# Batch 0's first layer and rows as streams of the scheduler, one bank fewer bound by attention, and a choice of engine for relu and for rows' copies

## The chip, the cores and the metric

The kernel runs on one core of a Trainium2 chip. The core has a matrix engine (TensorE, PE in the profile, with its weight load PEld), VectorE (DVE), ScalarE (ACT), GpSimd (POOL), and SyncE (SP), which here only sends DMAs. The metric is the device time of one execution in microseconds; shorter is better. The kernel before takes 310.22 us, the median of three runs from 309.73 to 310.73.

## The reference

Eight batches of eight heads, 576 positions, 64 features per head. First an attention with 32 landmarks (means of 18 neighbouring positions), whose inverse is found by six iterations; then, over the heads put side by side, a normalisation and a two-layer block with a residual:

```python
q_lm = q.reshape(B, H, m, S // m, D).mean(axis=3)      # k_lm alike, m = 32
A, Bm, C = sm(q, k_lm), sm(q_lm, k_lm), sm(q_lm, k)    # scaled softmax
Z = Bm.T / (norm1(Bm) * norminf(Bm) + 1e-6)
for _ in range(6):
    Z = 2 * Z - Z @ Bm @ Z
x = A @ Z @ C @ v                                      # then [B, S, 512]
xn = (x - mean(x)) / sqrt(var(x) + 1e-6) * g_ln
out = x + relu(xn @ w_ch1) @ w_ch2                     # 512 -> 2048 -> 512
```

## The kernel before

**Tiling.** A unit is four heads of one batch, so a batch has two. Per batch there are four kinds of TensorE work. *Attention* makes landmarks (`spread`, L805), scores, six iterations (`iterate`, L644) and the small products zt and zc. The *first layer* (`First`, L1077) never forms xn @ w1 from x: `product_of_heads` (L1085) multiplies zt by a quarter of w1 into two banks, VectorE or ScalarE evacuates them to `m16`, and each of 16 `chunk`s (L1108) multiplies `m16` by the exponentials `ea` into `psh`, from which relu writes the hidden activations `hT`. *Rows* (`rows_of`, L658) compute x itself, 128 positions at a time, into the tile `xblk`, of which twelve exist. The *second layer* (`second_layer`, L1151) accumulates 16 matmuls per block of 128 rows; `finish_block` (L1139) multiplies by the reciprocal deviation `rstd`, adds x, and the result is stored. Batches have 4.5 blocks, so `keep_tail` copies a half block into the next batch's `hT`.

**Weights.** w1 and w2 arrive in eight pieces each. w1 is scaled by g when it is cast (`scale_w1`, L351; by GpSimd or ScalarE), w2 is cast by GpSimd. The mean of x is taken out through w1: `less_mean` multiplies w1 by -1/512, which gives `less`; for batches 0 and 1 it is added while m is evacuated on VectorE, and `center_w1` later adds it to w1 for good.

**Order.** The program is straight-line. Every engine runs its own instructions in program order, so the order is decided when the program is written out. `Clock` (L72) models when each engine is free and when each tile is written. `run` (L1256) holds three generators, `attentions`, `first_layers` and `second_layers`. Each yields the time from which its next piece could start; the first in this order that is ready by now plus 60 ns goes next, else the earliest. Before each step `help_out` (L1190) hands out loads, GpSimd casts, VectorE's jobs for coming batches (`turn`, `add_up`, `turn_sums`), statistics (`measure`) and deviations (ScalarE), by how soon the engine is free; `LEAD` (L1188) is 700 ns. Attention of the first batch, and the whole of batch 0's first layer with its rows, the sums of w1, batch 1's preparation and blocks 0 and 1 of the second layer, are instead written out by hand at the end (L1304 to L1372), with fixed places by chunk number m. There, `warm` writes filler matmuls whose results nobody reads.

**PSUM.** `ps2` has two buffers of two banks each, which attention and `psh` share. Four more banks are handed out by `Banks` (L383) in rotation: `take` uses one, `hold` keeps it until `release`, and `next(k)` is the time when k of them are idle. By line 1355, `banks.order.remove(3)`, bank 3 leaves the rotation after batch 0's chunk 14, and `attention2` (L865) uses it for scores and iterations of all later batches.

**Engines.** `sooner` (L476) takes ScalarE or VectorE, whichever would end sooner by the model. Relu (L1115) and the copies of rows (L672) always go to ScalarE. Of a unit's q and k, the sums over positions come either from VectorE (`add_up`, for tiles named in `by_dve`) or from four adds on GpSimd while it casts, followed by a short `turn_sums` on VectorE.

## Time and profile before

| | us |
|---|---|
| median of 3 runs | 310.22 |
| the profiled execution | 311.25 |
| its span, first to last instruction | 309.5 |
| SyncE's issue of w2's eight pieces | 26.45 to 34.67 |
| first relu of batch 0, of batch 1 (start) | 27.97, 69.11 |
| end of the last relu | 281.22 |

The page splits the span into engines' busy shares, 40 slices, queues, the chain that ended last, and groups of instructions. A row of the timeline reads: start, length, engine, line, operation, output<-inputs, shape, count, and in brackets the idle time before it and what ended it. All scheduled operations stand under a helper's line (L221, L227), so they are told apart by tile names. The costliest groups, with busy us, mean ns, and the idle time ahead:

```
L227 PE MATMUL bank<-w,hT 128*128 128x512 f16 (+1 forms) x592 | 145.3, 376 | 2.9 <-DVE m L221 1.4
L221 ACT ACTIVATE hT<-psh 128x576 f16<-128x576 f32 x128 | 79.5, 655 | 27.6 <-PE psh L227 26.4
L227 PE MATMUL psh<-ea,m 128*128 128x288 f16 x512 | 81.9, 295 | 6.0 <-ACT hT L221 4.3
```

A matmul's length includes its latency; in a stream the 512-column ones follow each other every 0.216 us.

### The profile page before, as it was taken

The page shows a single profiled execution, that of the slowest core. Times are in us where ns is not written, and L with a number is a line of the kernel's source. Part 1 is how long each engine was busy: PE and PEld are TensorE (multiplying, and loading weights), DVE is VectorE, ACT ScalarE, POOL GpSimd, SP SyncE. Part 2 cuts the span into 40 slices and gives each one's busy share as a digit, 9 for nine tenths or more (in the row PEclk, how much of TensorE's full clock was granted, in tenths as well). Part 3 has the DMA queues.
Part 4 walks back from the last instruction along what each step waited for, and adds up shares of the span by engine and source line. Part 5 has one row for each costly group of instructions (what it writes and reads, how often), then busy time and mean ns, then how long its engine had stood idle before and what let it go on. Part 6 is the DMA issues. An engine that isn't in the chain of part 4 may idle for free.

```text
span 309.5 us, 8189 instructions
## 1 busy us (share of the span) xinstructions
PE 282.5 (91%) x3420; PEld 151.2 (49%) x3420; DVE 176.7 (57%) x388; ACT 173.4 (56%) x306; POOL 126.8 (41%) x156
## 2 busy tenths in 40 slices
PE   8988889979898999998899989789897999999995
PEld 8633554435543564544555544346443555465444
DVE  2645976979878877698758365544245221221112
ACT  2664855347753886369988746657552664473000
POOL 4387656999636999289920026100030000100000
PEclk9965999968999999999999999999999899999999
DMA  7999999979526699807801001210111111211343
GB/s 251 392 388 351 369 293 351 284 269 331 176 77 176 186 370 275 231 19 194 242 2 35 22 18 36 68 34 9 29 36 35 36 34 40 66 34 36 70 92 75
DMA packets 23485, 46.66 MB, mean 151 GB/s; under 512 B 2324, under 2 KB 2584, under 8 KB 23448
## 3 DMA queue, kind: packets, MB, share of 16 engines
q1 hardware_dynamic: 23288, 46.02, 48.6%
q8 instruction: 26, 0.43, 0.6%
q10 hardware_dynamic: 160, 0.13, 0.2%
q14 instruction: 11, 0.09, 0.1%
HBM read 36.70 MB, written 9.44 MB: 149 GB/s over the span
## 4 chain that ended last, share of the span: by engine, by line
PE 61%; DMA 17%; ACT 8%; DVE 5%; POOL 4%; issue 3%; SPq 1%; ACTq 0%; POOLq 0%
PE bank L227 40%; PE psh L227 16%; DMA wstg<-in_moe_w_ch_dram 8%; DMA out_dram<-xblk 4%; DMA stg<-in_q_dram 3%; ACT hT L221 3%; ACT xblk L221 2%; DVE xblk L221 2%; PE psd L227 2%; POOL asum L221 2%; DMA stg<-in_k_dram 2%; PE pscv L227 1%; ACT ec L221 1%; PE psec L227 1%; SPq L1047 1%
## 5 line engine op out<-in xcount | busy, mean ns | idle before, releaser
L227 PE MATMUL bank<-w,hT 128*128 128x512 f16 (+1 forms) x592 | 145.3, 376 | 2.9 <-DVE m L221 1.4
L221 ACT ACTIVATE hT<-psh 128x576 f16<-128x576 f32 x128 | 79.5, 655 | 27.6 <-PE psh L227 26.4
L227 PE MATMUL psh<-ea,m 128*128 128x288 f16 x512 | 81.9, 295 | 6.0 <-ACT hT L221 4.3
L227 PEld LDWEIGHTS <-hT 128*128 128x128 f16 x592 | 55.3, 98 | 55.5 <-issue 7.5
L227 PEld LDWEIGHTS <-m 128*128 128x128 f16 x512 | 49.2, 100 | 35.2 <-issue 12.3
L221 DVE SCALAR_TENSOR_TENSOR xblk<-bank,rstd,xblk 128x512 f32<-128x512 f32 (+1 forms) x37 | 27.1, 734 | 49.5 <-PE bank L227 48.1
L221 POOL TENSOR_TENSOR ea<-ea,lns 128x576 f16<-128x576 f16 x14 | 17.8, 1283 | 46.5 <-ACT lns L221 46.5
L221 POOL CAST nat<-stg 128x1152 f16<-128x1152 f32 x28 | 32.5, 1178 | 6.5 <-DVE xT L221 3.9
L221 POOL CAST natv<-stg 128x1152 f16<-128x1152 f32 x16 | 18.6, 1190 | 35.0 <-PE pscv L227 25.1
L221 ACT COPY xblk<-bank 128x512 f32<-128x512 f32 (+1 forms) x40 | 21.8, 592 | 19.3 <-DMA out_dram<-xblk 10.1
L221 DVE BATCH_NORM_STATS2 six<-xblk 128x6 f32<-128x512 f32 x36 | 24.4, 676 | 7.7 <-ACT xblk L221 7.6
L221 DVE CAST m<-bank 128x512 f16<-128x512 f32 x19 | 13.1, 691 | 24.4 <-PE bank L227 24.4
L221 DVE TENSOR_REDUCE part<-xT 128x32 f16<-128x576 f16 x32 | 22.9, 748 | 0.4
L221 ACT CAST m<-bank 128x512 f16<-128x512 f32 x29 | 16.4, 585 | 10.4 <-PE bank L227 10.4
L221 DVE STREAM_TRANSPOSE xT<-nat 128x576 uint32<-128x576 uint32 x28 | 21.5, 767 | 0.0
L227 PE MATMUL bank<-w,zt 64*32 64x512 f16 x256 | 15.9, 407 | 4.3 <-ACT xblk L221 4.0
L221 POOL COPY hT<-hT 128x1024 f16<-128x1024 f16 x4 | 4.1, 1037 | 37.8 <-PE bank L227 37.8
L227 PE MATMUL bank<-zcbd,ea 128*128 128x256 f16 (+1 forms) x80 | 15.6, 294 | 3.9 <-DVE xblk L221 2.0
L221 ACT ACTIVATE lns<-psd 128x576 f32<-128x576 f32 x16 | 10.3, 645 | 11.5 <-PE psd L227 11.4
L221 DVE SCALAR_TENSOR_TENSOR st<-st,bank 128x128 f16<-128x128 f16 (+2 forms) x36 | 11.1, 309 | 8.4 <-PE bank L227 8.4
L221 POOL TENSOR_TENSOR asum<-asum 128x256 f32<-128x256 f32 (+1 forms) x24 | 14.5, 604 | 1.9
L221 POOL TENSOR_TENSOR asum<-nat 128x512 f32<-128x512 f16 x12 | 14.5, 1207 | 1.0
(111 smaller groups left out, 262.3 us busy)
## 6 DMA issues: line engine op xcount, KB each, us to landing
stg<-in_q_dram SPq DMA_DIRECT2D x16, 576.0 KB, 6.0
stg<-in_k_dram SPq DMA_DIRECT2D x16, 576.0 KB, 6.9
out_dram<-xblk SPq DMA_DIRECT2D x70, 128.0 KB, 2.4
wstg<-in_moe_w_ch_dram SPq DMA_DIRECT2D x16, 512.0 KB, 8.0
stg<-in_v_dram SPq DMA_DIRECT2D x9, 576.0 KB, 7.7
stg<-in_v_dram SPq DMA_DIRECT2D x14, 288.0 KB, 7.8
out_dram<-xblk ACTq DMA_DIRECT2D x2, 64.0 KB, 2.2
out_dram<-xblk SPq DMA_DIRECT2D x2, 64.0 KB, 1.9
```

The costliest lines, as they stand in the source:

```text
L221: return lambda *args, **kw: keep(getattr(self.engine, op)(*args, **kw))
L227: keep(nc.tensor.matmul(o, l, r, start=start, stop=stop, tile_position=(rb, cb), skip_group_check=(skip or cb != 0)))
L1047: (nc.scalar if both and i else nc.sync).dma_start(out=to, in_=half)
```

## The change

Five things. (1) Batch 0's first layer is a generator (`first_layer0`) in `first_layers`, its rows are a fourth stream of `run` (between first and second layers), batch 1's preparation and attention go the way of all others, and blocks 0 and 1 of the second layer (`blocks_0_and_1`) are a piece of the second-layer stream, open once ten chunks are out. It waits for `hT` by the model, not for w2. The part written by hand goes. (2) `attention2` takes a bank from the rotation when it begins and releases it after its sixth iteration. Rows of batches from 1 on ask for two idle banks. (3) Relu, from batch 1 on, and those batches' copies of rows go to VectorE when the model has ScalarE later. (4) VectorE's lead is 400 ns until batch 1 is ready; statistics take precedence once a first layer has sent four chunks; deviations and the end of a block wait, by the model, for their inputs; k2's and k3's sums of batches 3 and 4 go to GpSimd, whose cast then also waits for a free `s16`. (5) In the opening a piece of w1 is scaled by VectorE one iteration later instead of by ScalarE, and there are more filler matmuls.

```diff
     heads, ready, multiplied, cast_v = {}, set(), {0}, {0}
+    rows0 = []
...
         st, bmT = softmax_of(psb, W)
-        warm(3, 256)
+        warm(4, 256)
...
-        cinv, _ = gram_of(p1([P, 4, W * LM], "psse"), st, bmT, W, lambda: warm(1, 256))
+        cinv, _ = gram_of(p1([P, 4, W * LM], "psse"), st, bmT, W, lambda: warm(2, 256))
...
-        warm(3, 256)
+        warm(4, 256)
         yield "gram"
...
         banks.release(*banks.held)
+        rows0.append(rows_of((0,), ea, zcbd_buf[0:2]))
         yield "zc"
-        yield from rows_of((0,), ea, zcbd_buf[0:2])
...
                 rows = ds(pb, n)
-                yield lambda: max(banks.next(), 0.0 if j in x_blk else xpool.next("xblk"),
+                yield lambda: max(banks.next(2 if b else 1), 0.0 if j in x_blk else xpool.next("xblk"),
                                   clock.at(ea[U * i], ea[U * i + 1], zcbd[U * i], zcbd[U * i + 1]))
...
                        zcbd[U * i + u][:].rearrange("p h d -> p (h d)"), cb=pb)
-                scalar.copy(xb[rows, :], psy[rows, :])
+                (sooner(512, clock.at(psy)) if b else scalar.copy)(xb[rows, :], psy[rows, :])
                 t0 += n
...
                 return max(clock.at(self.stg[i]), clock.idle(natv_buf[b % NV]))
-            return max(clock.at(self.stg[i]), nat.next("nat"))
+            return max(clock.at(self.stg[i]), nat.next("nat"),
+                       0.0 if nm + str(w) in self.by_dve else asm.next("s16"))
...
         W = len(units)
-        b3 = banks.tiles[3]
+        ecT, mine = {}, []
         def p1(shape, name):
-            return banks.view(3, shape)
-        psb = p1([P, W, LM], "psb")
-        ecT = {}
+            if not mine:
+                banks.hold([P, 512])
+                mine.append(banks.last)
+            return banks.view(mine[0], shape)
         for y in range(W // 2):
             pair = (2 * y, 2 * y + 1)
-            yield lambda: max(clock.idle(b3) if y == 0 else 0.0, ps2.next("p2", 2), aexp.next("e", 4),
+            yield lambda: max(0.0 if mine else banks.next(), ps2.next("p2", 2), aexp.next("e", 4),
                               clock.at(c.lm_tile[y], *[xT["k", w] for w in pair]))
+            if y == 0:
+                psb = p1([P, W, LM], "psb")
             for w in pair:
...
                 it += 1
+                if it == 6:
+                    banks.release(mine[0])
             else:
...
             o = self.hT[:, m, ds(64 * (self.b % 2), S)].rearrange("p (a t) -> p a t", a=2)
-            act(o, psh[:, :, 0:HS], AF.Relu)
+            at = clock.at(psh)
+            if self.b and max(clock.free["Activation"], at) + 650 > max(clock.free["DVE"], at) + 810:
+                dve.tensor_scalar(out=o, in0=psh[:, :, 0:HS], scalar1=0.0, scalar2=None, op0=ALU.max)
+            else:
+                act(o, psh[:, :, 0:HS], AF.Relu)
...
         l1 = First(b)
+        if b == 0:
+            yield from first_layer0(l1)
+            return
         yield lambda: max(banks.next(2), mprod.next("m16"), clock.at(l1.zt))
...
             l1.chunk(m)
+            if m == 3:
+                begun_first[0] = b
             if m % 4 == 0 and m < 12:
...
             asm.unpin(l1.zt)
+    chunks0 = [0]
+    def first_layer0(l1):
+        l1.product_of_heads(0)
+        scale_w1(5, 1, scalar)
+        for m in range(MCH):
+            yield lambda: max(ps2.next("p2"), clock.at(l1.m16[m // 4], *l1.ea))
+            l1.chunk(m)
+            chunks0[0] = m + 1
+            if m == 0:
+                scale_w1(7, 1, scalar)
+            if m in (2, 6):
+                f = 2 if m == 2 else 3
+                for c in range(KCH):
+                    yield lambda: max(0.0 if c else banks.next(), clock.at_key(w1_16[:, c, ts(f, 512)]))
+                    if c == 0:
+                        psf_of[f] = banks.hold([P, 512])
+                        mine = banks.last
+                    MM(psf_of[f][:], lesser[:], w1_16[:, c, ts(f, 512)], start=(c == 0),
+                       stop=(c == KCH - 1))
+                scalar.copy(less(f), psf_of.pop(f)[:])
+                banks.release(mine)
+            if m in (1, 5, 9):
+                yield lambda: max(banks.next(2), mprod.next("m16"))
+                l1.product_of_heads(m // 4 + 1)
...
+    def finished(b):
+        while b not in rstds:
+            if blocks_done.get(b) == 4 + b % 2:
+                yield lambda: clock.at(stats_of[b])
+                deviations(b)
+            elif unmeasured:
+                measure()
+            else:
+                yield lambda: 0.0 if b in rstds or unmeasured else NEVER
+        yield lambda: clock.at(rstds[b])
+    def blocks_0_and_1():
+        yield lambda: banks.next(2) if chunks0[0] >= 10 else NEVER
+        accs = []
+        for u in range(2):
+            accs.append((banks.hold([P, DM]), banks.last))
+        for m in range(MCH):
+            yield lambda: clock.at_key(hTs[0][:, m, 0:P]) if chunks0[0] > m else NEVER
+            for u in range(2):
+                MM(accs[u][0], hTs[0][:, m, ts(u, P)], w2_16[:, m, :],
+                   start=(m == 0), stop=(m == MCH - 1))
+        yield from finished(0)
+        for u in range(2):
+            finish_block(0, u, accs[u][0])
+            banks.release(accs[u][1])
     def second_layer(b):
         hT = hTs[b]
+        if b == 0:
+            yield from blocks_0_and_1()
         blocks = range(4 + b % 2) if b else (2, 3)
...
                        start=(m == 0), stop=(m == MCH - 1))
-                while b not in rstds:
-                    if blocks_done.get(b) == 4 + b % 2:
-                        deviations(b)
-                    elif unmeasured:
-                        measure()
-                    else:
-                        yield lambda: 0.0 if b in rstds or unmeasured else NEVER
+                yield from finished(b)
                 if u == blocks[-1]:
...
     sets = [Coming((1,), ("k0", "k1", "q0", "q1"))]
-    sets += [Coming(bs, [f"k{w}" for w in range(U * len(bs))]) for bs in ((2,), (3, 4), (5, 6), (7,))]
-    LEAD = 700
+    sets += [Coming(bs, [f"k{w}" for w in range(U * len(bs))] if bs != (3, 4) else ["k0", "k1"]) for bs in ((2,), (3, 4), (5, 6), (7,))]
+    def lead():
+        return 700 if 1 in ready else 400
...
                     break
-            if clock.free["DVE"] <= now + LEAD:
+            if clock.free["DVE"] <= now + lead():
                 mine = [c for c in sets if c.jobs][:1]
-                if unmeasured and current[0] >= group_of(unmeasured[0])[0]:
+                if unmeasured and begun_first[0] >= group_of(unmeasured[0])[0]:
                     measure()
...
                     begun = -1
-                elif mine and mine[0].job_ready() <= now + LEAD:
+                elif mine and mine[0].job_ready() <= now + lead():
                     mine[0].next_job()
...
             b = current[0]
-            if b not in rstds and blocks_done.get(b) == 4 + b % 2:
+            if (b not in rstds and blocks_done.get(b) == 4 + b % 2
+                    and clock.at(stats_of[b]) <= now + 200):
                 deviations(b)
...
-    current = [0]
+    current, begun_first = [0], [0]
     def attentions():
-        yield from a1
-        for c in sets[1:]:
+        for c in sets:
             for y in range(len(c.units) // 2):
...
     def first_layers():
-        for b in range(1, B):
-            yield lambda: 0.0 if (b in ready and current[0] == b - 1
-                                  and (b <= LAST_WHOLE or len(centered) == 4)) else NEVER
+        for b in range(B):
+            yield lambda: 0.0 if b == 0 or (b in ready and current[0] == b - 1
+                                            and (b <= LAST_WHOLE or len(centered) == 4)) else NEVER
             yield from first_layer(b)
             first_done.add(b)
+            if b == 0:
+                keep_tail(0)
...
     def run():
-        streams = [attentions(), first_layers(), second_layers()]
+        streams = [attentions(), first_layers(), rows0[0], second_layers()]
         waits = [next(g) for g in streams]
...
             at = [w() if w else 2 * NEVER for w in waits]
-            k = next((k for k in range(3) if at[k] <= now), None)
+            k = next((k for k in range(4) if at[k] <= now), None)
             if k is None:
...
         next(a0)
-        if it == 0:
-            scale_w1(1, 1, scalar)
+        if it == 1:
+            scale_w1(1, 1, dve)
         if it < 2:
-            warm(2, 192)
+            warm(3, 256)
+        elif it < 4:
+            warm(1, 256)
         if it == 3:
...
     next(a0)
-    l1 = First(0)
-    l1.product_of_heads(0)
-    scale_w1(5, 1, scalar)
-    accs = [banks.view(u, [P, DM]) for u in range(2)]
-    def blocks_0_and_1(m):
-        for u in range(2):
-            MM(accs[u][:], hTs[0][:, m, ts(u, P)], w2_16[:, m, :],
-               start=(m == 0), stop=(m == MCH - 1))
-    a1 = attention2((1,), b1)
-    for m in range(MCH):
-        l1.chunk(m)
-        if m == 0:
-            scale_w1(7, 1, scalar)
-        if m == 1:
-            l1.product_of_heads(1)
-        if m == 2:
-            less_mean(2)
-        if m == 5:
-            l1.product_of_heads(2)
-        if m == 6:
-            less_mean(3)
-        if m == 8:
-            l1.product_of_heads(3)
-        if m == 9:
-            banks.order, banks.held = [3, 2, 0, 1], {0, 1}
-        if m in (7, 8, 10, 11, 12, 13):
-            next(a0, None)
...
-        if m == 13:
-            b1.spread(0)
-        if m == 14:
-            assert not b1.jobs
-            banks.order.remove(3)
-            next(a1)
-            next(a1)
-        help_out()
-        if m >= 10:
-            blocks_0_and_1(2 * (m - 10))
-            blocks_0_and_1(2 * (m - 10) + 1)
-    keep_tail(0)
-    next(a1)
-    for m in range(12, MCH):
-        blocks_0_and_1(m)
...
     run()
```

More of the change, by code (lines that the diff above doesn't have):

```diff
@@ L1317 @@
     next(a0)
-    l1 = First(0)
-    l1.product_of_heads(0)
-    scale_w1(5, 1, scalar)
-    accs = [banks.view(u, [P, DM]) for u in range(2)]
-    def blocks_0_and_1(m):
-        for u in range(2):
-            MM(accs[u][:], hTs[0][:, m, ts(u, P)], w2_16[:, m, :],
-               start=(m == 0), stop=(m == MCH - 1))
-    a1 = attention2((1,), b1)
-    for m in range(MCH):
-        l1.chunk(m)
-        if m == 0:
-            scale_w1(7, 1, scalar)
-        if m == 1:
-            l1.product_of_heads(1)
-        if m == 2:
-            less_mean(2)
-        if m == 5:
-            l1.product_of_heads(2)
-        if m == 6:
-            less_mean(3)
-        if m == 8:
-            l1.product_of_heads(3)
-        if m == 9:
-            banks.order, banks.held = [3, 2, 0, 1], {0, 1}
-        if m in (7, 8, 10, 11, 12, 13):
-            next(a0, None)
-        if 2 <= m < 10:
-            b1.next_job()
-            if b1.jobs and b1.jobs[0][0] == b1.add_up and b1.jobs[0][2]:
-                b1.next_job()
-        if m == 13:
-            b1.spread(0)
-        if m == 14:
-            assert not b1.jobs
-            banks.order.remove(3)
-            next(a1)
-            next(a1)
-        help_out()
-        if m >= 10:
-            blocks_0_and_1(2 * (m - 10))
-            blocks_0_and_1(2 * (m - 10) + 1)
-    keep_tail(0)
-    next(a1)
-    for m in range(12, MCH):
-        blocks_0_and_1(m)
-    while 0 not in rstds:
-        if unmeasured:
-            measure()
-        deviations(0)
-    for u in range(2):
-        finish_block(0, u, accs[u])
-    banks.release(0, 1)
     run()
```

## The prediction

> **What bounds the kernel now.** I first read the busy shares by engine and the granted clock over 40 slices, then the chain of work that ended last.

> ```profile
> PE 282.5 (91%) x3420; PEld 151.2 (49%) x3420; DVE 176.7 (57%) x388; ACT 173.4 (56%) x306; POOL 126.8 (41%) x156
> PEclk9965999968999999999999999999999899999999
> PE 61%; DMA 17%; ACT 8%; DVE 5%; POOL 4%; issue 3%; SPq 1%; ACTq 0%; POOLq 0%
> ```

> TensorE is busy 91% of the span and carries 61% of the chain. The last stretch of the chain, 25.3 us from 280.5, is second-layer matmuls only, and no part of the change shortens it. But busy isn't full speed: the clock row falls to 0.5 to 0.6 in slices 3 and 4 and again near slice 9. The answer with windows of one microsecond places this: 0.50 from 17.4 to 30.6 us, from 65.0 to 71.6, and from 239.5 to 242.8. So the gain must come from TensorE's waits and from the half-clock stretches behind them. The table of waits (engine, who released it, total, times, longest) names them:

> ```profile
> PE bank L227 <- ACT xblk L221: 5.6, 7, 1.5
> PE psh L227 <- ACT hT L221: 4.3, 10, 1.3
> PE bank L227 <- DVE xblk L221: 2.5, 2, 2.0
> PE bank L227 <- DVE m L221: 1.4, 1, 1.4
> PE psd L227 <- ACT ea L221: 1.3, 1, 1.3
> ```

> These are rows' copies, relu, the finishing of a block, the products' evacuation, and one exponential in the opening. The change touches each of them. The timeline of TensorE shows the three waits ahead of the three clock drops:

> ```profile
> 17.73 0.64 PE L227 MATMUL psd<-ea,bones 128*128 128x288 f16 x2 [1.27 <-ACT ea L221]
> 65.36 2.75 PE L227 MATMUL bank<-zcbd,ea 128*64 128x256 f16 x10 [1.96 <-DVE xblk L221]
> 237.39 0.41 PE L227 MATMUL bank<-w,zt 64*32 64x512 f16 x7 [1.49 <-ACT xblk L221]
> ```

> **The clock, by row and by rule.** All three drops follow a wait of 1.27 to 1.96 us. [...] By the row, the 6.6 us at half rate goes too, worth up to 3.3 us more. I go by the row: [...]the clock fell three times.

> **a. Opening, up to 45.5 us.** ScalarE scales a piece of w1 (0.72 us at 16.42) after waiting 0.87 us for its DMA, and the exponential that TensorE needs stands behind it. That scaling goes to VectorE. No VectorE row has it: below, a 128x1152 fp32 cast takes 0.76 us, so 512 columns some 0.34; above, GpSimd's row for the same scaling, 0.74. I take 0.5, nearer the cast. It can't start before the piece lands at 16.4, so VectorE is free at 16.9, and the third iteration's update (0.29), which is queued behind it, ends at 17.2 instead of 16.4. TensorE's fourth iteration then starts near 17.25, not 18.30: 1.0 us won. The added filler matmuls are 4,608 columns against 2,560: 2,048 more, 0.85 us at 2.4 columns per ns, which the 512-column rows 0.216 us apart show. Most falls into waits on VectorE; I charge 0.3. How much survives? The weights decide: GpSimd's last cast of w2 runs from 44.47 to 45.51, and the DMA share is about 1.0 from 10 to 60 us. At 45.57 TensorE still had two or three chunks (0.49 each) and half of the 32 matmuls of blocks 0 and 1 to do (16 x 0.216 = 3.5), so being earlier can pay at most about 3. Since `blocks_0_and_1` doesn't test w2 before it puts a matmul into TensorE's queue, TensorE may wait there instead, and batch 1's attention behind it; the casts come 1.2 to 2.4 us apart. Bounds -1 to 3, taken 1.0.

> **b. The gap at 63 us.** Batch 0's work runs out before batch 1 is ready. Three banks rotate: two hold the products sent at 63.00, one the last block of batch 0, and the fourth is attention's for good. Rows of batch 1 so wait for VectorE's xblk (64.57 to 65.31). With attention's bank given back after the sixth iteration (60.55) they need only zcbd (63.91 to 64.65): 0.66 us. The rest must come from batch 1 being ready sooner. VectorE idles 1.76 us before 26.10 and 1.76 before 29.52, while batch 1's first k is cast by 27.34; its transpose and two sums (0.77 + 1.42) now go by readiness and fill most of the second hole. The shorter lead (400 ns for 700) keeps about one job fewer ahead of each of the six updates, which stood about 1.5 us apart from 53.34 to 60.97. Together 1.5 to 2.5 us. With the clock, bounds 0.7 to 5.3 (1.96 + 3.3), taken 3.5.

> **c. Relu by the sooner engine.** Where no second-layer work is left to interleave, ScalarE sets the pace:

> ```profile
> 140.00:150.00 10.00, 8.64 (x68) 5.06 (x68) 8.07 (x15) 9.55 (x19) 9.68 (x12) 1.00 0.78 251
> 150.00:160.00 10.00, 8.65 (x113) 4.96 (x111) 6.34 (x15) 9.13 (x18) 6.29 (x9) 1.00 0.32 73
> ```

> (Columns: TensorE, weight load, VectorE, ScalarE, GpSimd busy us, clock, DMA.) From 146.65 to 157.9 there are 15 chunks, 0.75 us each, against 0.49 of TensorE each and three products of 0.35: a floor of 8.4 us, so at most 2.8 is to be had. A relu on VectorE: its casts out of PSUM take 0.29, 0.43 and 0.69 us for 128, 256 and 512 columns, 1.04 ns per column, so 0.76 for 576, beside ScalarE's 0.655. A quarter of the chunks moved takes the pace to about 0.6: 2.2 us. In batch 1's stretch (70 to 80 us) VectorE is itself full (9.49 of 10), so nothing moves there. Behind a waiting relu stand m's evacuations on VectorE. Bounds -0.5 to 2.8, taken 2.0.

> **d. Four banks and rows' copies, 190 to 252 us.** In ScalarE's timeline a copy waits for a store to free its slot:

> ```profile
> 199.22 0.58 ACT L221 COPY xblk<-bank 128x512 f32<-128x512 f32 x1 [1.99 <-DMA out_dram<-xblk]
> 208.24 0.59 ACT L221 COPY xblk<-bank 128x512 f32<-128x512 f32 x1 [1.86 <-DMA out_dram<-xblk]
> 236.75 0.58 ACT L221 COPY xblk<-bank 128x512 f32<-128x512 f32 x1 [3.58 <-DMA out_dram<-xblk]
> ```

> TensorE's products, which need that bank, wait 1.29, 1.19 and 1.49 us. A fourth bank lets them go on, and rows that start only with two banks idle leave one over. But the store still lands about 2.4 us after it is sent, and relus and m's casts stay behind the blocked copy on ScalarE unless VectorE takes them. At stake: 5.6 us of waits and half of the 3.3 us window, 7.2. Less than half is taken: 3.0.

> **e. Two k sums to GpSimd.** For batches 3 and 4 the sums of k2 and k3 leave VectorE. GpSimd's four adds take 1.21 + 0.75 + 0.45 + 0.43 = 2.84 us, VectorE's two reductions 1.50. [...] By the trace, GpSimd idles 5.47 us ahead of 88.38, just after the two tiles are cast (80.68 to 82.9), which covers nearly all of 5.7, while VectorE is packed from 94 to 112 and sheds 2 x (1.50 - 0.50) = 2.0. If that hole is gone, q's casts and batch 3 are late by up to 5.7. Taken 0.5. The statistics' new order and the new waits ahead of ScalarE's deviations save part of its 3.6 us of waits for stats; cover is ample, so nothing is counted.

> **Sum.** 1.0 + 3.5 + 2.0 + 3.0 + 0.5 = 10.0, less 1.0 for VectorE's queue getting longer and new orders colliding: 9.0. The profiled execution took 311.25 us (span 309.5, 1.75 around it), so 302.25; its median beside it is 310.22, 1.03 lower, so **301.2**.

> **Rivals.** *Everything closes (18%).* The upper bounds are 3 + 5.3 + 2.8 + 7.2 + 2 = 20.3; three quarters give 15: 295. For it speaks that one cause, a short wait, also takes the clock; against it that a new order brings waits of its own.
> *Hidden anyway (18%).* The weights' arrival fixes the opening, VectorE fixes batch 1's readiness, and relu seldom moves since ScalarE is faster when both are free (0.655 against 0.76): the change then does little of what it says. Left are 0.7 in b and about 0.5 each in c and d: 1.7, so 308.5.
> *VectorE's queue blocks (19%), slower.* Rows' copies sent to VectorE take the waits for stores along: ScalarE had 10.1 us of them in 5. On VectorE they would stand ahead of the block finishes (0.75), which free second-layer banks and start the very stores that are waited for. Where over half of the 10.1 us lands there, each us is TensorE's: about 10 lost, 6 won: 314. It decides once VectorE waits for out_dram over some 6 us in all. For it: ScalarE runs 8 copies in a row at 142.2, which the rule of choice would spread. Against it: slots are tested before the matmul is sent.

> **Numbers.** The forecast's own case (45%) spans 298 to 305. Under 0.3% (0.93 us) can't be told from no change. Faster: 45 + 18 + 11 of the hidden case's 18 = 74; the same: 7; slower: 19. The range reaches from 294 to 311.5, with some 8% below and 12% above.

> **What would show it.** a: no wait for ea near 17, and a clock of 1.0 from 17 to 30. b: no gap of 1.9 us near 63 and no half clock behind it. c: relu rows on VectorE, and under 0.65 us per chunk in batch 3's first layer. d: TensorE's waits for xblk under 3 us. e: no later start of batch 3's first layer than 138.8. I am wrong if TensorE waits on w2 or if VectorE waits on stores.

## The result and the profile after

The changed kernel takes 306.63 us, the median of 11 runs (304.70 to 309.55), beside 310.61 us for the kernel before (11 runs). The ratio is 0.987 (95% interval 0.984 to 0.990): faster by 4.0 us, where 9.0 were forecast. A ratio is taken between the means of the executions that lie within 1.5% of the fastest of their kernel (all but one of these 22), so it can differ a little from the ratio of the medians. The profiled execution took 305.81 us, with a span of 304.1.

First the page of the changed kernel: busy shares, the granted clock over 40 slices, and the shares of the chain.

```profile
PE 277.5 (91%) x3429; PEld 150.5 (49%) x3429; DVE 186.1 (61%) x407; ACT 162.7 (53%) x287; POOL 131.2 (43%) x164
...
PEclk9997998699999999977999999999999999999999
...
PE 62%; DMA 14%; POOL 9%; ACT 5%; DVE 5%; issue 3%; SPq 1%; POOLq 0%; ACTq 0%; DVEq 0%
```

TensorE bounds the kernel as before. The 0.5 of the opening is gone from the clock row and so is the dip near 240 us, but there is a new pair of 7s in slices 18 and 19 (130 to 145 us), and the dip before batch 1 stays. TensorE's waits:

```profile
PE bank L227 <- DVE st L221: 6.0, 3, 5.4
PE pscv L227 <- POOL s L221: 3.0, 1, 3.0
PE psh L227 <- ACT hT L221: 2.5, 7, 0.9
PE psh L227 <- DVE hT L221: 1.8, 4, 0.7
...
PE bank L227 <- DVE xblk L221: 1.1, 2, 0.7
```

The wait for ScalarE's xblk, 5.6 us before, is gone. Two waits stand at the top that the kernel before has at 0.4 us and at 1.0 at most: 5.4 us for `st` and 3.0 us for `pscv`. The next table shows where time went. It adds, over windows of 10 us, TensorE's idle time and its busy time multiplied by one minus the granted clock (filler matmuls count as busy, and the changed kernel has more of them in the opening; the tail after the last matmul is left out):

| lost by TensorE, us | 0-50 | 50-100 | 100-150 | 150-200 | 200-250 | 250-290 |
|---|---|---|---|---|---|---|
| before | 12.4 | 7.3 | 2.7 | 4.1 | 6.0 | 1.1 |
| changed | 8.4 | 7.9 | 7.7 | 2.5 | 2.6 | 0.0 |

So TensorE lost 4.0 us less in the opening and 6.1 less after 150 us, and 5.6 more between, nearly all of it from 100 to 150. Each row is one execution: ten runs below that have the changed kernel's order of TensorE up to there lose 7.9 to 9.7 us from 0 to 50, so a difference of about 1 us in this table says little. The start of each batch's first layer says the same: batch 1 at 67.9 before and 68.5 after, batch 3 at 140.9 and 145.6, batch 6 at 239.6 and 232.9. Rows of the windows (TensorE, weight load, VectorE, ScalarE, GpSimd busy, clock, DMA share, GB/s), the kernel before first:

```profile
0.00:50.00 50.00, 43.55 (x537) 25.92 (x537) 30.63 (x75) 28.97 (x46) 29.09 (x54) 0.86 0.99 339
...
100.00:150.00 50.00, 47.30 (x721) 25.39 (x719) 39.62 (x86) 35.95 (x66) 41.24 (x46) 1.00 0.72 223
```

and the changed kernel:

```profile
0.00:50.00 50.00, 42.98 (x554) 27.13 (x555) 29.45 (x71) 28.45 (x47) 31.99 (x57) 0.97 1.00 348
...
100.00:150.00 50.00, 44.63 (x675) 23.32 (x674) 36.36 (x82) 27.63 (x50) 30.90 (x35) 0.93 0.55 168
```

From 0 to 50 us the clock rises from 0.86 to 0.97. From 100 to 150 TensorE is busy 2.7 us less at a lower clock, and GpSimd 10.3 us less.

**The first new wait.** The timeline of the changed kernel:

```profile
46.81 1.16 POOL L221 CAST natv<-stg 128x1152 f16<-128x1152 f32 x1 [1.52 <-DMA stg<-in_v_dram]
47.92 1.04 POOL L221 COPY hT<-hT 128x1024 f16<-128x1024 f16 x1
...
50.09 0.78 DVE L221 STREAM_TRANSPOSE xT<-nat 128x576 uint32<-128x576 uint32 x1 [6.44 <-POOL nat L221]
...
52.23 0.21 DVE L221 TENSOR_REDUCE rsum<-bank 128x2 f32<-128x64 f32 x1
...
52.96 0.21 PE L227 MATMUL bank<-st,bones 128*128 128x64 f16 x1 [5.39 <-DVE st L221]
```

VectorE waits 6.44 us with a transpose for batch 2, whose cast on GpSimd stands behind casts that wait for v and behind the copy of `hT`. The scheduler's estimate had put that transpose into VectorE's queue; batch 1's softmax (from 52.23) is behind it, and TensorE's next step behind that.

**The second.** TensorE's product of batches 3 and 4 is 144 small matmuls. In the kernel before, and then in the changed one:

```profile
129.87 0.51 PE L227 MATMUL pscv<-natv,ecT 64*32 64x65 f16 x43 [0.55 <-issue]
```

```profile
130.10 0.88 PE L227 MATMUL pscv<-natv,ecT 64*32 64x65 f16 x72
...
134.02 0.81 PE L227 MATMUL pscv<-natv,ecT 64*32 64x65 f16 x72 [3.04 <-POOL s L221]
```

The view names a sum on GpSimd, but it may be merely the event that came last: the tiles that these 72 read were all long written (the last `natv` by 123.46, the last `ecT` by 127.14), and the weight load beside them stood still as well. Instructions are the suspect: a packet of 16,384 bytes of the kind "instruction" lands at 132.53, 1.5 us before TensorE goes on.

### The profile page after: what moved, and what is told of

Same layout as the page of the kernel before. It is cut to its first block, busy times and chain, and to the rows that moved or that the text cites. A ratio compares the mean times of both kernels' runs of the same rounds, so it can differ in the third digit from the quotient of the medians.

```text
span 304.1 us, 8214 instructions
## 1 busy us (share of the span) xinstructions
PE 277.5 (91%) x3429; PEld 150.5 (49%) x3429; DVE 186.1 (61%) x407; ACT 162.7 (53%) x287; POOL 131.2 (43%) x164
## 4 chain that ended last, share of the span: by engine, by line
PE 62%; DMA 14%; POOL 9%; ACT 5%; DVE 5%; issue 3%; SPq 1%; POOLq 0%; ACTq 0%; DVEq 0%
PE bank L227 41%; PE psh L227 16%; DMA stg<-in_v_dram 6%; DMA wstg<-in_moe_w_ch_dram 5%; POOL nat L221 2%; POOL asum L221 2%; ACT hT L221 2%; POOL natv L221 2%; DMA stg<-in_k_dram 2%; DMA out_dram<-xblk 2%; PE pscv L227 2%; DVE xblk L221 1%; PE psd L227 1%; DVE hT L221 1%; POOL w L221 1%
## 5 line engine op out<-in xcount | busy, mean ns | idle before, releaser
L227 PE MATMUL bank<-w,hT 128*128 128x512 f16 (+1 forms) x592 | 146.5, 380 | 0.0
L227 PEld LDWEIGHTS <-hT 128*128 128x128 f16 x592 | 55.4, 98 | 54.6 <-issue 8.0
L221 ACT ACTIVATE hT<-psh 128x576 f16<-128x576 f32 x111 | 69.4, 653 | 24.0 <-PE psh L227 22.8
L227 PE MATMUL psh<-ea,m 128*128 128x288 f16 x512 | 77.8, 288 | 4.7 <-ACT hT L221 2.5
L227 PEld LDWEIGHTS <-m 128*128 128x128 f16 x512 | 48.9, 98 | 29.8 <-issue 9.9
L221 DVE SCALAR_TENSOR_TENSOR xblk<-bank,rstd,xblk 128x512 f32<-128x512 f32 (+1 forms) x37 | 26.9, 730 | 37.8 <-PE bank L227 34.0
L221 POOL TENSOR_TENSOR ea<-ea,lns 128x576 f16<-128x576 f16 x14 | 17.9, 1288 | 40.9 <-ACT lns L221 40.9
L221 POOL CAST nat<-stg 128x1152 f16<-128x1152 f32 x28 | 31.6, 1144 | 8.3 <-DVE xT L221 6.5
L221 ACT COPY xblk<-bank 128x512 f32<-128x512 f32 (+1 forms) x35 | 19.8, 587 | 20.6 <-DMA out_dram<-xblk 9.5
L221 POOL CAST natv<-stg 128x1152 f16<-128x1152 f32 x16 | 18.2, 1161 | 27.1 <-PE pscv L227 16.7
L221 DVE BATCH_NORM_STATS2 six<-xblk 128x6 f32<-128x512 f32 x36 | 24.5, 681 | 5.4 <-ACT xblk L221 5.4
L221 DVE STREAM_TRANSPOSE xT<-nat 128x576 uint32<-128x576 uint32 x28 | 21.5, 767 | 7.7 <-POOL nat L221 7.3
L221 ACT CAST m<-bank 128x512 f16<-128x512 f32 x32 | 18.0, 591 | 6.8 <-PE bank L227 6.8
L221 DVE CAST m<-bank 128x512 f16<-128x512 f32 x16 | 11.0, 690 | 16.7 <-PE bank L227 16.0
L221 DVE TENSOR_REDUCE part<-xT 128x32 f16<-128x576 f16 x28 | 20.2, 745 | 0.3
L221 ACT ACTIVATE lns<-psd 128x576 f32<-128x576 f32 x16 | 10.3, 646 | 15.4 <-PE psd L227 15.3
L221 POOL COPY hT<-hT 128x1024 f16<-128x1024 f16 x4 | 4.2, 1038 | 32.8 <-PE bank L227 32.8
L221 POOL TENSOR_TENSOR asum<-asum 128x256 f32<-128x256 f32 (+1 forms) x28 | 17.2, 615 | 2.2
L221 DVE TENSOR_SCALAR hT<-psh 128x576 f16<-128x576 f32 x17 | 12.8, 755 | 7.9 <-PE psh L227 7.6
L227 PE MATMUL bank<-zcbd,ea 128*128 128x256 f16 (+1 forms) x80 | 14.9, 284 | 2.8 <-DVE xblk L221 1.1
L221 POOL TENSOR_TENSOR asum<-nat 128x512 f32<-128x512 f16 x14 | 16.5, 1177 | 1.1
L221 DVE SCALAR_TENSOR_TENSOR st<-st,bank 128x128 f16<-128x128 f16 (+2 forms) x36 | 11.2, 312 | 8.6 <-PE bank L227 8.5
```

The source lines that it names most:

```text
L221: return lambda *args, **kw: keep(getattr(self.engine, op)(*args, **kw))
L227: keep(nc.tensor.matmul(o, l, r, start=start, stop=stop, tile_position=(rb, cb), skip_group_check=(skip or cb != 0)))
```

## The experiments

Each run is compared with the kernel before, run beside it; the changed kernel's ratio is 0.987. All but the three named before_... start from the changed kernel.

**1. The first wait taken away.**

```diff
-elif mine and mine[0].job_ready() <= now + lead():
+elif (mine and (mine[0] is sets[0] or 1 in softmaxed)
+      and mine[0].job_ready() <= now + lead()):
```

> Edit: VectorE's transposes and sums for batch 2 and later are held back until batch 1's softmax is in VectorE's queue. Theory 1 (batch 0's gain of 8 us is lost because batch 1's softmax stands in VectorE's queue behind batch 2's first transpose, which waits 6.44 us for a GpSimd cast): TensorE's wait for st of 5.39 us before 52.96 goes to under 1 us, the half clock after it goes, batch 1's first layer starts near 63 instead of 68.5, and the time falls by 3 to 6 us, to 301 to 304. Rival (batch 1's start is not what counts, since second-layer work and batch 2's readiness fill up the difference): the wait goes, but the time stays within 1.5 us of 306.6. Third possibility (batch 2 pays: its jobs come later and its first layer starts later than 97.7): slower than 306.6.

Measured: 307.72 us, ratio 0.993 (0.989 to 0.996). The wait is gone and batch 1's first layer starts at 64.4 instead of 68.5, but batch 2's at 106.0 instead of 97.7: the third possibility. ScalarE's copy of batch 2's landmarks, in the changed kernel and then here:

```profile
69.27 0.60 ACT L221 CAST lm<-bank 128x512 f16<-128x512 f32 x1
```

```profile
91.80 0.59 ACT L221 CAST lm<-bank 128x512 f16<-128x512 f32 x1 [12.95 <-PE bank L227]
```

In this run VectorE does statistics and the centering of w1 from 67 to 86 us, and batch 2's last transposes only at 85.94 to 90.40: the rules of precedence put both ahead of them. Experiment 7 comes back to it.

**2. Parts undone.** Relu always on ScalarE:

```diff
-if self.b and max(clock.free["Activation"], at) + 650 > max(clock.free["DVE"], at) + 810:
+if False:
```

> Edit: relu always on ScalarE again, the rest as changed. If relu by the sooner engine is worth the 2.0 us forecast: slower than the changed kernel by 1 to 3 us, with the first layers of batches 3, 5 and 7 longer by 1 to 3 us each (before: 16.7, 18.6, 13.8; changed: 14.5, 14.3, 12.6). Rival (17 of 128 relus moved, ScalarE is no longer the pace since its queue is free of blocked rows' copies): within 0.8 us of 306.6.

Measured: 307.77 us, ratio 0.993 (0.990 to 0.995), so relu is worth some 0.54% or 1.7 us. The first layers of batches 3, 5 and 7 take 15.8, 20.9 and 13.8 us, against 14.5, 14.3 and 12.6 in the changed kernel. Batches 3 and 7 are as theory one has it; batch 5's 6.6 us more is far outside it, and that batch also starts 4.1 us sooner.

Attention's bank kept for good:

```diff
-                if it == 6:
-                    banks.release(mine[0])
```

> Edit: attention keeps its bank for good again, so three banks rotate; the rest as changed. If the fourth bank makes the gain after 200 us: TensorE's waits for xblk out of ScalarE come back (over 3 us in all, 0 in the changed kernel), and the time rises by 3 to 6 us, to 310 to 313, with the loss after 200 us. Rival (the late gain comes from relu and the new order of streams): within 1.5 us of 306.6.

Measured: 313.28 us, ratio 1.010 (1.006 to 1.013). The waits for ScalarE's xblk are back with only 1.9 us of 5.6, and the loss isn't late: batch 3 starts at 156.6, 11 us later, while the stretch from 200 to 250 us loses 3.1 us, against 2.6 in the changed kernel and 6.0 in the kernel before. The loss after 200 us that was expected is hardly there. The last chunk of batch 7 ends at 280.4 against 274.2.

The sums of k2 and k3 back on VectorE:

```diff
-Coming(bs, [...] if bs != (3, 4) else ["k0", "k1"])
+Coming(bs, [...])
```

> Edit: the sums of k2 and k3 of batches 3 and 4 are VectorE's again, the rest as changed. If that move delays batch 3 (its first layer starts at 145.6 instead of 140.9, GpSimd waits 10.5 us for a free buffer of halved sums): batch 3 starts near 141 to 143 and the time falls by 1 to 4 us. Rival (batch 3's delay comes from statistics and relus that go ahead on VectorE): batch 3's start stays at 144 to 147, or gets later by up to 2, and the time is the same or up to 1.5 us longer.

Measured: 312.43 us, ratio 1.009 (1.005 to 1.012). Neither theory: batch 3 starts at 148.2, and the loss is 6.6 us, not up to 1.5. The sums on GpSimd aren't what delays batch 3.

Rows' copies on ScalarE alone:

```diff
-(sooner(512, clock.at(psy)) if b else scalar.copy)(xb[rows, :], psy[rows, :])
+scalar.copy(xb[rows, :], psy[rows, :])
```

> Edit: rows' copies on ScalarE only, the rest as changed (5 of 40 copies ran on VectorE in the changed kernel). If the choice of engine is part of the late gain: TensorE waits again for xblk out of ScalarE by over 2 us after 190 us, time 1 to 3 us longer. Rival (the fourth bank does it, the choice hardly ever falls on VectorE): within 1 us of 306.6.

Measured: 308.32 us, ratio 0.993 (0.990 to 0.995): 0.54% for 5 copies. No wait of TensorE for xblk out of ScalarE came back; the stretch from 50 to 100 us loses 1.7 us more and 200 to 250 us 0.6. A size of theory one without its mechanism, and neither loss is clear of the scatter between executions.

The opening as before (fillers, and the piece of w1 on ScalarE):

```diff
-        if it == 1:
-            scale_w1(1, 1, dve)
+        if it == 0:
+            scale_w1(1, 1, scalar)
```

> Edit: the opening's filler matmuls and the scaling of the piece of w1 by ScalarE as before the change, the rest as changed. In the changed kernel TensorE lost 8.4 us to idling and low clock in the first 50 us, before it 12.4. If the 4 us count to the end: slower than 306.6 by 2 to 4 us. If they end in the wait for st of 5.4 us before 52.96, since VectorE's queue fixes the start of batch 1: half clock is back near 17 to 30 us, batch 1's first layer starts within 1 us of 68.5 and the time is within 1 us of 306.6.

Measured: 307.07 us, ratio 0.991 (0.988 to 0.995), about 1.3 us and at the edge of what can be told. The half clock comes back only in part (0.91 from 10 to 30 us), and TensorE's wait for the exponential with 1.4 us. TensorE's wait for `st` before batch 1 is 6.5 us and batch 1's first layer starts at 69.9, both inside what the runs with the new opening show (4.1 to 7.3 us, 68.4 to 70.0): what the opening wins doesn't reach batch 1.

The statistics by the old rule:

```diff
-if unmeasured and begun_first[0] >= group_of(unmeasured[0])[0]:
+if unmeasured and current[0] >= group_of(unmeasured[0])[0]:
```

> Edit: the statistics of finished blocks go ahead on VectorE by the old rule (by the batch whose second layer runs), the rest as changed. If the new precedence delays batches 3 and 4 (VectorE did statistics at 100 to 107 us while GpSimd waited 10.5 us for a buffer of halved sums): batch 3's first layer starts near 141 to 143 instead of 145.6, and the time falls by 1 to 3 us. Rival (VectorE is full there whichever goes first): within 1 us of 306.6, or later batches are slowed by up to 2 us since their relus and deviations wait.

Measured: 306.81 us, ratio 0.991 (0.987 to 0.994). Batch 3's first layer starts at 141.0, as theory one has it, and GpSimd's wait for a buffer of halved sums falls from 10.5 to 4.7 us; yet nothing is won: the 0.4% to the changed kernel isn't clear of the scatter. TensorE now stops just ahead of the product and in it, 1.54 and 3.24 us. So the new statistics rule, to which the forecast gave no price, is one cause of batch 3's delay. That the product's stall takes what the old rule would give is a guess here; experiment 5 tests it.

**3. Is the second wait a lack of instructions?** Two edits of its surroundings. In the first, 32 tiny matmuls stand ahead of everything:

```diff
+for _ in range(32):
+    MM(shifting[:, 0:16], zeros[:, 0:P], zeros[:, 0:16])
```

> Edit: 32 tiny matmuls on zeros (64 instructions) ahead of everything else on TensorE, where it waits for the first load; the order of the rest is the same. Theory (blocks of 256 instructions): the stall in the product of batches 3 and 4 moves from its 73rd to its 41st matmul, the one that is now instruction 3266, and takes 1.5 to 3 us; the second (187.8 us) moves by 32 matmuls as well or goes. Rival (the stall is a wait for data or a semaphore): it stays ahead of the 73rd matmul of the product. Time: within 2 us of 306.6 by both.

Measured: 310.00 us, ratio 0.999 (0.997 to 1.002); the time is 3.4 us longer than the changed kernel's 306.63, more than both theories allowed. Batch 0's first layer starts 3.2 us later; the tiny matmuls themselves put off the first transposes by 0.55, and where the rest comes from was not followed up. What matters is the place of the stall, in this run's timeline:

```profile
132.66 0.48 PE L227 MATMUL pscv<-natv,ecT 64*32 64x65 f16 x40
...
135.51 1.05 PE L227 MATMUL pscv<-natv,ecT 64*32 64x65 f16 x104 [2.36 <-issue]
```

It stands behind the 40th matmul now, not the 72nd: in the same place of TensorE's instruction stream, 64 instructions earlier in the work. Counting the stream (each matmul, each weight load and each of TensorE's few semaphore records is one), the gap lies at instruction 3265 or 3266 in every kernel here but one (before_bank, below), in the kernel before too (0.75 us), though often at another matmul of the product. Further gaps lie at 3010, 3522 and 4802, multiples of 256 away. And each of them ends 1.2 to 1.6 us after an instruction packet has landed.

In the second edit, the product is cut in four parts:

```diff
+since[0] = clock.now() + 900
```

> Edit: after each quarter of an attention's product (40 or 32 of the small 64x65 matmuls) the next quarter may not be issued for 900 ns, so that other matmuls come between. In the changed kernel TensorE stands still for 3.04 us before 134.02 and 0.96 us before 187.80, each time between its instructions 3265 and 3266 or 4801 and 4802 of its stream. Theory (TensorE runs out of instructions: a block of 256 is fetched by one 16,384-byte packet, and a burst of 144 small matmuls eats a block faster than the next one comes): the stall at instruction 3266 falls below 1 us, the half clock behind it (2.4 us) goes, and the time falls by 2 to 5 us, to about 302 to 304.5. Rival (the stall is a wait for data, or batch 3 is bound by VectorE anyway): time within 1 us of 306.6.

Measured: 305.44 us, ratio 0.987 (0.983 to 0.990), as the changed kernel. The gap at 3266 stays (3.10 us), and 3522 adds 1.54. That missed theory one: with other matmuls between the parts the block ahead lasts 3.8 us without the gap instead of 2.8, but its packet starts 4.46 us after the block begins instead of 3.46. So the burst of small matmuls alone doesn't set the gap; the delay of the packet does.

**4. Why is the packet late?** The loads of batches 5 and 6 are sent from 96.0 to 123.0 us in the kernel before and from 110.6 to 131.6 in the changed one. First the cause of that delay was tried: six buffers of halved sums.

```diff
-tag="s16", bufs=4)
+tag="s16", bufs=6)
```

> Edit: six buffers instead of four for GpSimd's halved sums, the rest as changed. In the changed kernel GpSimd stands 10.5 us (to 111.64) for one of them, so the loads of batches 5 and 6 run at 110 to 133 us (before: 96 to 125), on top of the product of batches 3 and 4. If that wait delays batch 3 and brings the loads onto the instruction packet: GpSimd's wait falls below 4 us, batch 3's first layer starts at 140 to 143 instead of 145.6, the stall at instruction 3266 falls from 3.2 to about 1 us, and the time falls by 2 to 5 us. Rival (VectorE's queue is the limit, GpSimd only waits in its place): wait moves, batch 3 starts at 144 or later, time within 1 us of 306.6.

Measured: 311.96 us, spread from 307.74 to 316.06 over 22 executions, ratio 1.002 (0.998 to 1.005), which is 1.5% above the changed kernel's. The rival has the waits right, not the time. In the profiled execution, one of the longer ones (312.83 us), GpSimd's 10.5 us for a buffer are gone and its waits for VectorE's transposes rise from 6.5 to 13.6; loads are still sent until 131.9 us, the gap at 3266 is 3.7 us, and batch 3 starts at 147.9, no sooner.

Then loads and casts of batches 5 and 6 were held back until the product is issued.

```diff
+if not (held_back[0] and c.bs == (5, 6)) and ...
```

> Edit: loads and casts of batches 5 and 6 are held back from the spread of batches 3 and 4 until their product has been issued, the rest as changed. Theory (an instruction packet waits behind bulk loads: with loads at 230 to 415 GB/s it starts 2 to 4.5 us after TensorE begins the block ahead, without loads 0.2 to 0.9): no loads at 120 to 133 us, the packet for instruction 3266 starts within 1 us, and TensorE's gap there is under 1.3 us instead of 3.2; the time falls by 1 to 4 us if batches 5 and 6 bear the delay. Rival (the packet is late for another reason[...]): the gap stays at 2.5 us or more.

Measured: 313.92 us, ratio 1.013 (1.009 to 1.018), but the gap at 3266 falls to 0.53 us and the packet starts 0.87 us after TensorE begins the block ahead. The loads, let go from 130 us on, meet the next packet instead: at 297 GB/s of loads ahead of it, TensorE stands 2.4 us at instruction 3522. More time is lost elsewhere, as this run's timeline shows:

```profile
134.42 1.15 POOL L221 CAST nat<-stg 128x1152 f16<-128x1152 f32 x1 [10.55 <-DMA stg<-in_k_dram]
...
147.07 2.52 POOL L221 TENSOR_TENSOR ea<-ea,lns 128x576 f16<-128x576 f16 x2
...
149.08 0.40 PE L227 MATMUL pszt<-st,cv 32*64 32x32 f16 x16 [9.79 <-ACT lns L221]
```

The casts, released too early, stand in GpSimd's queue ahead of batch 3's normalisation, and TensorE waits 9.8 us for that. So only the loads beyond the first four were held back, and until the attention ends; TensorE's order is that of the changed kernel, matmul by matmul but for a few pairs that start together.

```diff
+if not (held_back[0] and c.bs == (5, 6) and len(c.loads) <= 8) and ...
```

> Edit: only the loads of batches 5 and 6 beyond the first four are held back, from the spread of batches 3 and 4 until their attention ends; TensorE's order stays that of the changed kernel. If loads delay the instruction packet and the loss at 100 to 150 us is this stall: loads at 122 to 133 us are gone, the packet for TensorE's instruction 3266 starts within 1.2 us of the block ahead (changed kernel: 3.46), the gap there falls from 3.2 to 0.5 to 1.3 us, the half clock behind it goes, and the time falls by 2 to 5 us, to 302 to 304.5. Rival (what is won is given back, since batches 5 and 6 are prepared later or other work sets their start): the gap falls, the time stays within 1 us of 306.6 or rises.

Measured: 302.14 us, ratio 0.974 (0.971 to 0.977): 1.3% under the changed kernel, about 4 us, as theory one has it. The stretch from 100 to 150 us loses 3.4 us less, and batch 3's first layer starts at 141.3 instead of 145.6. The product in this run:

```profile
130.67 0.75 PE L227 MATMUL pscv<-natv,ecT 64*32 64x65 f16 x72
...
132.08 0.75 PE L227 MATMUL pscv<-natv,ecT 64*32 64x65 f16 x72 [0.66 <-POOL nat L221]
```

The DMA view of 128 to 131.4 us, the changed kernel and then this run (queue and kind: packets, MB, share of 16 engines):

```profile
DMA packets 645, 1.40 MB, mean 411 GB/s; under 512 B 38, under 2 KB 38, under 8 KB 645
...
q1 hardware_dynamic: 645, 1.40, 104.5%
```

```profile
DMA packets 74, 0.16 MB, mean 46 GB/s; under 512 B 4, under 2 KB 4, under 8 KB 73
...
q1 hardware_dynamic: 73, 0.14, 17.2%
q8 instruction: 1, 0.02, 2.2%
```

(A packet counts with all its time in the window in which it starts, so a share can pass 100%.) With 16 engines full of loads no instruction packet starts in these 3.4 us; without them one does. Beside it the row of 100 to 150 us, to be held against the two above:

```profile
100.00:150.00 50.00, 47.26 (x707) 25.52 (x705) 39.12 (x89) 31.33 (x57) 31.70 (x36) 0.97 0.51 153
```

| | loads in the 2 us ahead, GB/s | packet starts after the block ahead began, us | gap at 3266, us |
|---|---|---|---|
| before | 233 | 2.06 | 0.75 |
| changed | 415 | 3.46 | 3.23 |
| shift | 410 | 3.70 | 2.56 |
| opening_old | 411 | 2.81 | 3.23 |
| split | 401 | 4.46 | 3.10 |
| hold | 0 | 0.87 | 0.53 |
| loads_late | 32 | 0.88 | 0.86 |
| before_bank | 132 | -0.69 | none |

(The 2 us are those ahead of the packet. The gap is counted from the start of the matmul ahead of it, which makes it 0.2 us longer than the idle time in the timeline's brackets.) The rate of loads isn't all: in bank_kept the packet starts 4.32 us after the block ahead began, at 245 GB/s, and the gap is 4.59 us. The gap follows from the packet's start and from how fast TensorE uses up the block ahead: in the changed kernel 3.46 us to the packet, 1.07 of transfer and 1.48 until TensorE goes on, less the block's own 2.80, leave 3.21.

Most packets start only when TensorE has begun the block ahead: 36 of the 53 in the profiles of the kernel before and the changed one. Such a packet has no more than the time that TensorE takes for that block: 2.8 us in the changed kernel, with the product's matmuls in it.

**5. Both: later loads and the old statistics rule.**

> Edit: the same, and the statistics by the old rule, which let batch 3 start at 141.0 instead of 145.6 without a gain in time. If the stalls for instructions were what took that gain: the two gaps there (1.5 and 3.2 us) fall below 1.3 each and the time falls to 300 to 303.5. Rival: the stalls go and the time stays at 305 to 307, since the later batches hang on VectorE.

Measured: 305.98 us, ratio 0.988 (0.985 to 0.991). The rival came true: the gap at 3266 is 1.17 us, so the stall isn't what took the old rule's gain; batch 3 starts at 135.0, 6 us sooner than in loads_late, and takes 22.2 us instead of 15.4; the stretches from 150 to 250 us lose 9.6 us, where loads_late loses 4.4. A batch that starts sooner isn't a kernel that ends sooner.

**6. Parts alone, in the kernel before.** The bank given back:

> Edit: the kernel before, with one part of the change alone: attention takes a bank when it starts and gives it back after its sixth iteration. Undoing this part of the changed kernel cost 7 us (2.3%). If the parts add up: 303 to 305 here, 5 to 7 us under the kernel before. If its worth in the changed kernel comes from the other parts (second layer and rows that start by readiness and need two idle banks): 0 to 3 us under the kernel before.

Measured: 314.88 us, ratio 1.017 (1.012 to 1.021). The sums on GpSimd:

> Edit: the kernel before, with one part of the change alone: GpSimd makes the sums of k2 and k3 of batches 3 and 4, and its casts test for a buffer of halved sums first. Undoing it in the changed kernel cost 6.6 us (2.1%). If that is its own worth: 303 to 305. If it is worth the 0.5 us of the forecast, and the 6.6 us came from a new order of everything behind it: within 1.5 us of the kernel before, to either side.

Measured: 317.49 us, ratio 1.021 (1.014 to 1.027); here the product's gap at 3266 is 4.0 us and the one at 3010 1.5. Relu by the sooner engine:

> Edit: the kernel before with relu by the sooner engine alone. Undoing it in the changed kernel cost 1.7 us (0.54%). If its worth is its own: 307.5 to 309 where the kernel before takes about 310. Rival (any new order of the kernel before costs, as with the bank alone, 5 us, and the sums alone, 6.6 us): 311 to 316.

Measured: 309.97 us, ratio 0.998 (0.994 to 1.001). Alone, the bank costs 5.2 us and the sums 6.4, where undoing them within the change costs 7.0 and 6.6. The parts don't add up. The likeliest reading, argued and not shown, is that each edit gives the scheduler a new order, and that where loads, VectorE's jobs and the product then meet decides more than the part itself. Why the bank alone costs 5 us isn't settled: it takes TensorE's waits for ScalarE's xblk from 5.6 us to 0.2, as was meant, but waits for relu rise from 4.3 to 8.8.

**7. The first wait again.** As in experiment 1, and batch 2's jobs ahead of statistics and of the centering of w1:

```diff
+if mine and mine[0] is sets[1] and 1 in softmaxed and mine[0].job_ready() <= now + lead():
+    mine[0].next_job()
```

> Edit: as in the run first (VectorE's jobs for batch 2 and later held back until batch 1's softmax is in its queue), and then batch 2's jobs go ahead of statistics and of the centering of w1. If the wait of 5.4 us costs its time once batch 2 is kept on time: batch 1's first layer starts at 63 to 65 instead of 68.5, batch 2's at 92 to 97.7 (first: 106.0), and the time falls by 2 to 5 us, to 302 to 304.5. Rival (TensorE is earlier there but waits for loads or VectorE before batch 3): batch 1 and 2 start sooner, batch 3 at 144 to 147 as before, time within 1 us of 306.6.

Measured: 303.93 us, ratio 0.979 (0.976 to 0.982), 0.8% or 2.5 us under the changed kernel. From its timeline:

```profile
46.86 0.19 PE L227 MATMUL bank<-st,bones 128*128 128x64 f16 x1
...
63.37 1.17 PE L227 MATMUL psh<-ea,m 128*128 128x288 f16 x4
```

The wait of 5.39 us at 52.96 is gone, and batch 1's first layer starts 5.1 us sooner, batch 2's 2.3. The product of batches 3 and 4 still waits 3.75 us for "issue" here; in the next run it is 0.58.

With the later loads as well:

> Edit: first2 and the later loads of batches 5 and 6 together. If both losses are independent: 297 to 301. If batch 3's start is set by VectorE and GpSimd and not by TensorE: 301 to 303, no better than the later loads alone (302.1).

Measured: 299.05 us, ratio 0.965 (0.960 to 0.969). It beats both kernels: 2.3% under the changed one. Its page:

```profile
PE 273.4 (92%) x3425; PEld 147.4 (50%) x3425; DVE 185.5 (63%) x408; ACT 162.0 (55%) x286; POOL 132.1 (45%) x164
...
PEclk9999999979999999999999999999999999999999
```

By the same sum TensorE loses 6.0, 6.8, 4.4, 1.5, 2.1 and 0 us in the six stretches, 20.8 in all against 29.1 in the changed kernel. The two edits win 2.5 and 4.0 us alone and 7.0 together: within the scatter they add up, as two independent losses would.

## Why the prediction was wrong

The direction was right, the size was off by 5.0 us: 306.63 lies above the 298 to 305 of the forecast's own case. Two terms failed, b, and the 1.0 us for collisions; a came out about as forecast, c's size came out with half of its mechanism, and d's signs came true without its cause being shown. By the steps:

**a, forecast 1.0:** undoing it costs some 1.3 us, within the error of it. The fourth iteration starts at 17.34 us, where 17.25 was forecast, the exponential's wait is gone and the clock is 1.00 from 10 to 20 us and 0.83 from 20 to 30, not yet 1.0. That half clock, from 23.9 to 27.3 us, follows waits of TensorE of 0.53 us and less, 1.6 us idle in the 4 us from 20 to 24: the forecast was right to go by the rows of the trace. TensorE lost 4.0 us less in the first 50, but what stopped that gain wasn't the weights, which the forecast took to decide (no wait for w2 shows). It was the wait of step b, which ends when VectorE's queue lets it, with the old opening as with the new.

**b, forecast 3.5, failed.** The step said "The rest must come from batch 1 being ready sooner". Batch 1 started 0.6 us later (0.5 to 2.1 later in the nine runs with the same order up to there), and the stretch from 50 to 100 us lost no less. The short wait near 63 us went; one of 5.39 us came at 52.96, with 6.8 us of half clock. The shorter lead was counted as fewer jobs ahead of the updates; that one job could enter VectorE's queue on an estimate and stand there for 6.44 us was not. first and first2 show it: without it batch 1 starts 4.1 and 5.1 us sooner, and the time falls by 2.5 us once batch 2 is kept on time.

**c, forecast 2.0:** about 1.7 where undone, 17 of 128 relus on VectorE at 0.755 us each, for which 0.76 was estimated. But the named sign failed: from the second to the last chunk of batch 3's first layer TensorE takes 0.73 us per chunk, where 0.76 was the pace before and under 0.65 was forecast. There relu gives 0.4 us of the 2.2 counted; in batch 7 it gives 1.2, and batch 5 is shorter in another order of work. That the size fits is in part luck. Alone it is 0.7, not to be told from nothing.

**d, forecast 3.0:** TensorE's wait for ScalarE's xblk went from 5.6 us to nothing, the dip at 240 us is gone, and the stretch from 200 to 250 lost 3.4 us less. That the bank can take this wait away is shown by before_bank (0.2 us left). But what won the 3.4 us stays open: with the bank kept for good that stretch loses only 0.5 us more, with rows' copies on ScalarE 0.6; both undone together were not run. The rival of VectorE's blocked queue didn't come: 9.5 us of waits for stores stayed on ScalarE, and VectorE has none.

**e, forecast 0.5:** the named sign, no later start of batch 3 than 138.8, failed: 145.6. But the cause wasn't e. It was the statistics' order, of which the prediction said "nothing is counted", and the loads: the old rule brings batch 3 to 141.0, the later loads bring it to 141.3, and both to 135.0. Undoing e costs 6.6 us, and e alone in the kernel before costs 6.4, with a gap of 4.0 us in the product there; no price of two reductions against four adds explains either. That it is the new order of everything is argued, not shown.

**The term for collisions, forecast 1.0, failed.** The sum has no place for 100 to 150 us, where 5.0 us were lost. It takes off "1.0 for VectorE's queue getting longer and new orders colliding", and this collision alone, TensorE's instruction packet against the loads, cost about 4.0. The kernel before showed a trace of it, `pscv` waiting 0.55 and 0.98 us for "issue", which the forecast passed over. Taking the loads away from that place, with TensorE's order kept, gives 4.0 us: the stall is 2.4 us shorter and 0.8 us of low clock goes. With both losses taken out the kernel takes 299.05 us, 2.2 under the forecast of 301.2. So these two collisions are more than what was missing; but the two edits are changes of their own, and their sum doesn't show that each gain counted in c, d and e is there.

## What to carry to other kernels

When a scheduler written out by hand gets freedom, price the places where its estimate can be wrong: a job that enters an in-order queue before its input is there blocks all behind it (here VectorE for 6.44 us, and through it TensorE for 5.39), so put the chain that TensorE waits for ahead of jobs for later batches. Look at a stall that no operand explains by its place in the instruction stream; if such stalls lie multiples of 256 instructions apart, as here at 3010, 3266, 3522 and 4802, and bulk loads run there (415 GB/s ahead of the packet for 3266), move the loads: here that won about 4 us. Don't add up parts that were measured one at a time, undone or alone.
